# Prices and ranks of a hand-planned schedule: attention with mixed heads, then a squared-ReLU FFN

## The chip, the core and the metric

The kernel runs on one core of a Trainium2 chip. The core has a matrix engine (PE, with its weight loads shown as PEld), a vector engine (DVE), a scalar engine (ACT), a general engine (POOL), a queue engine that mostly issues DMAs (SP), and 16 DMA engines. Each engine works through its own instructions strictly in the order in which the program lists them, and waits at an instruction until its inputs and its buffers are there. The metric is the device time of one execution in microseconds; less is better.

## The reference

```python
scores = scale * np.matmul(q, k.transpose(0, 1, 3, 2))        # batch 8, heads 12, seq 448, head_dim 64
scores = np.einsum('bhij,hg->bgij', scores, w_pre)
scores = scores - np.max(scores, axis=-1, keepdims=True)
attn = np.exp(scores)
attn = attn / (np.sum(attn, axis=-1, keepdims=True) + 1e-09)
attn = np.einsum('bhij,hg->bgij', attn, w_post)
out = np.matmul(attn, v)
...
x = out.transpose(0, 2, 1, 3).reshape(B * S, H * D)           # 3584 x 768
h = np.maximum(x @ w_in, 0.0)                                 # 3584 x 2048
y = h * h @ w_out                                             # 3584 x 768
```

Heads are mixed before the softmax by w_pre (12 x 12) and after it by w_post. Then each of the 3584 tokens goes through a two-layer FFN with a squared ReLU.

## The kernel before

**Tiling.** Attention runs batch by batch. The 448 rows of a batch are cut into 45 chunks of about 10 query rows times 12 heads, so that a chunk fills 120 partitions. A chunk needs, in this order: a mix product of the scores with the w_pre pattern (L801, or L807 for the chunks of the first batch that mix q instead), a minimum on DVE (L812), an exponential on ACT (L815), a reciprocal on DVE (L821), a scaling of the w_post pattern on POOL (wq, L824), four products that both mix back and transpose (L831), and an eviction into `atb` by DVE or ACT (L485 or L487). Before that stand the scores (L679), their eviction into `snat`, and a DMA on SP that lays them out by chunk in `sch`. After it, the products with v (L876) fill `xt`.

**FFN.** Two batches share a block of 896 tokens, which is worked in units of 256 or 128 tokens. The first layer (L933, `mms` in `unit`) takes six products for each 128 hidden columns; DVE (L947) or ACT (L951) does the ReLU into `hr`; POOL squares it into `h2` (L954, at the rank FILL). The second layer (L972) takes 16 products for each group of 128 tokens and 384 output columns, in four pieces of four products; the groups are evicted into `osb`, of which there are two, and stored by SP (L996).

**The plan.** `Planner` simulates the engines while the program is built and writes down the order in which each picks its operations; that order is the program's. An operation has a price in ns for each engine that may do it, a rank `pri` (lower goes first) and dependencies. An engine that comes free takes the ready operation of lowest rank. Attention work ranks by chunk number (`n`), scores and relayouts ahead of it by AHEAD, most FFN work at FILL = 1e6, so that the FFN fills what attention leaves. An operation with two engines goes to whichever comes free first. Only the order reaches the chip; a price that differs from the chip's time makes an order that waits there.

**Near copies.** From the third batch on, q and k are loaded by POOL's DMAs into `qs` and `ks` (`load`, price 750), copied by `near` on POOL or DVE into `qn` and `kn` with the heads of a pair side by side (L610; `x_piece` makes six copies for each of two pieces of a batch, 72 in all), and then transposed by a DMA that SP issues (turn_k L623, turn_q L629) into the slots `kt` and `qz` that the scores read. A turn also waits until the slot's former scores are done. The copies rank `b * NCHUNK - 24 + 4.5 * g`, that is 24 chunks before their batch.

**Idle products.** At the start PE does products on zeros (L1183) where the plan leaves it idle, so that its clock stays up. They are planned before 9 us, and until 130 us wherever the planner's model of the clock is slow, or where PE's share of the last 3413 ns is under IDLE_LOW. The landings of the first loads of k, q and the last rows of q are planned by `first`, with a count of rows and ns a row.

Of the kernel before, what the change touches and what calls it, by code (L numbers as in the profile page):

```python
# [17 lines left out]
FT = DFF // 128  # L18
# [17 lines left out]
P_KEYS = S // NB  # L36
W2B = 2 * S
NSLOT = 2
NEAR, TURN_SP = {"POOL": 1000, "DVE": 270}, 1500
PIECE = NPAIR // 2  # L40
NE = 6
NSCH = 11
AHEAD = 7.4
FIFO = 50
IDLE_NS, IDLE_COLS, IDLE_FROM, IDLE_END, IDLE_LOW = 112, 256, 1300, 130000, 0.55
SPELL, PHASE, DROP, RISE = 3413, 1700, 0.4, 0.8
ROWS, COLS = 1, 2
TURN = 95
LATER = 2
GS, ONE = [(0, 1, 2)], [(0,), (1,), (2,)]  # L50
STAY = {ROWS: 2, COLS: 6}
HOLD = "g"
# [24 lines left out]
SOON = 0  # L77
# [42 lines left out]
class Planner:  # L120
# [8 lines left out]
    def add(self, eng, ns, pri, fn, deps=(), lat=60, bank=None, frees=None, mode=0):  # L129
        op = Op(eng if isinstance(eng, dict) else {eng: ns}, lat, pri, fn, list(deps), bank, frees, mode)  # L130
        self.ops.append(op)
        return op
# [169 lines left out]
def kernel(  # L302
# [189 lines left out]
    add = pl.add  # L492
    FILL = 1e6
    slots = {}
# [3 lines left out]
    def load(rows, each, pri, fn, deps):  # L498
        if len(loads) >= 7:
            deps = list(deps) + [loads[-7]]  # L500
        op = add("POOL", 750, pri, fn, deps, lat=850)
        done = pl.moved("LOAD", rows, each[0], each[1], 0, [op], 1500)
        loads.append(done)
        return done

    q_in, k_in, v_in = {}, {}, {}
    def keep(key, fn):
        def go(*got):
            for key_, slot in zip(key if isinstance(key, list) else [key], got):
                slots[key_] = slot  # L510
            fn(*got)
        return go
# [12 lines left out]
    h_op, sq_op, o_op, st_op = {}, {}, {}, {}  # L525
# [81 lines left out]
    tq_op, tk_op = {}, {}  # L607
# [4 lines left out]
    def x_piece(b, g):  # L612
        i = (2 * b + g) % NSLOT
        h0 = 2 * PIECE * g

        def pair_k(eng, a):
            near(eng, kn[:, :, 2 * a:2 * a + 2, :], ks[:, h0 + 2 * a:h0 + 2 * a + 2, :, :].rearrange("p h j d -> p j h d"))

        def pair_q(eng, a):
            near(eng, qn[:, :, 2 * a:2 * a + 2, :], qs[:, h0 + 2 * a:h0 + 2 * a + 2, :, :].rearrange("p h r d -> p r h d"))  # L620

        def turn_k():
            nc.sync.dma_start(  # L623
                out=kt[i][:, :, :, :].rearrange("p j a c -> p (j a) c"),
                in_=kn[:, :, :, :].rearrange("p j h d -> p (j h d)"), transpose=True,
            )

        def turn_q():
            nc.sync.dma_start(  # L629
                out=qz[i][:, :, :, :].rearrange("p r a c -> p (r a) c"),  # L630
                in_=qn[:, :, :, :].rearrange("p r h d -> p (r h d)"), transpose=True,
            )

        pri = b * NCHUNK - 24 + 4.5 * g
        old = used(b, g)
        ck = [
            add(NEAR, 0, pri, lambda eng, a=a: pair_k(eng, a), [k_in[b, g], tk_op.get(2 * b + g - 1)], lat=80)
            for a in range(PIECE)
        ]
        cq = [  # L640
            add(NEAR, 0, pri, lambda eng, a=a: pair_q(eng, a), [q_in[b, g], tq_op.get(2 * b + g - 1)], lat=80)
            for a in range(PIECE)
        ]
        sk = add("SP", 2300 if b == 2 else TURN_SP + 300, pri, turn_k, ck + old)
        sq = add("SP", 2000 if b == 2 else TURN_SP + 100, pri, turn_q, cq + old)
        k_ = tk_op[2 * b + g] = add("TURN", 1500, pri, lambda: None, [sk], lat=6000)
        q_ = tq_op[2 * b + g] = add("TURN", 1200, pri, lambda: None, [sq], lat=6000)
        for p in range(PIECE * g, PIECE * g + PIECE):
            ready[b, p] = [[k_]] + [[k_, q_]] * NJ
            got_op[b, p] = ck + cq  # L650
# [16 lines left out]
    def score(b, r, group):  # L667
# [13 lines left out]
        first = TAIL_FIRST if b == 0 and r == 0 else C0[r]  # L681
        pri = b * NCHUNK + first - AHEAD - 0.6 - (0.7 if r == 0 else 1.4) * (NPAIR - p)
        n = b * (NJ + 1) + r - 2
# [232 lines left out]
    def unit(pair, ui):  # L916
        a, z = units_of(pair)[ui]
        w = z - a
        nf = 512 // w
        ix = len(units)  # L920
        units.append((pair, ui))
        h2_ = h2[ix % 2]
        fill = FILL + 100 * ix
# [3 lines left out]
        prev = None  # L927
        for f0 in range(0, FT, nf):
            key = ("f", ix, "h", f0)
            for j in range(nf):  # L930
                def mms(slot, f0=f0, j=j):
                    for c2 in range(NPAIR):
                        nc.tensor.matmul(  # L933
                            slot[:, j * w:(j + 1) * w], lhsT=w1[c2][:, (f0 + j) * 128:(f0 + j + 1) * 128],
                            rhs=xt[:, c2, a:z], start=(c2 == 0), stop=(c2 == NPAIR - 1),
                        )
                if j == 0:
                    prev = add("PE", w * 2.55, fill + f0, keep(key, mms), xdeps + w1_in + [prev], lat=0, bank=key)
                else:
                    prev = add("PE", w * 2.55, 0, lambda key=key, mms=mms: mms(slots[key]), [prev], lat=0)  # L940
# [23 lines left out]
        for mt in range(w // 128):  # L964
            whole = not (z == W2B and mt == 1 and pair == B // 2 - 1)
            cuts = [0, 384, DMODEL] if whole else [0, 384, 640, DMODEL]
            for nt, (c0, c1) in enumerate(zip(cuts, cuts[1:])):
                key = ("f", ix, "o", mt, nt)
                for f0 in range(0, FT, 4):
                    def mms(slot, f0=f0, mt=mt, c0=c0, c1=c1):  # L970
                        for ft in range(f0, f0 + 4):
                            nc.tensor.matmul(  # L972
                                slot[:, 0:c1 - c0], lhsT=h2_[:, ft, mt * 128:(mt + 1) * 128],
                                rhs=w2[:, ft, c0:c1],
                                start=(ft == 0), stop=(ft == FT - 1),
                            )
                    if f0 == 0:
                        prev = add("PE", 12 + (c1 - c0) * 5 // 3, fill + 20 + 4 * mt + 2 * nt, keep(key, mms),
                                   [prev] + sq_op[ix][0:4 // nf] + w2_in[0:1 if ix < SOON else 4], lat=0, bank=key)
                    else:  # L980
                        prev = add("PE", 12 + (c1 - c0) * 5 // 3, FILL, lambda key=key, mms=mms: mms(slots[key]), [prev, w2_in[f0 // 4]] + sq_op[ix][0:(f0 + 4) // nf], lat=0)
                    o_op[ix].append(prev)
                end = add("WAIT%s" % str(key), 0, 0, lambda: None, [prev], lat=200)
                si = ix_store[0]

                def evac(eng, key=key, si=si, c0=c0, c1=c1):
                    copy(eng, osb[si % 2][:, c0:c1], slots[key][:, 0:c1 - c0])

                ev = add({"DVE": 80 + (c1 - c0) * 25 // 24, "ACT": 165 + (c1 - c0) * 5 // 7}, 0, 0, evac, [end, st_op.get(si - 2)] + ([m_op[n_] for n_ in direct] if si < 2 else []), lat=100, frees=key)
                evs = evs + [ev] if nt == 1 and whole else [ev]  # L990
                if nt == 1 or not whole:
                    done = []
                    for rows, dst, o in pieces(pair, a + mt * 128, None if whole else (c0, c1)):
                        side_ = not whole and rows <= CI
                        def store(dst=dst, o=o, rows=rows, si=si, e0=0 if whole else c0, e1=DMODEL if whole else c1, eng=nc.scalar if side_ else nc.sync):
                            eng.dma_start(out=dst, in_=osb[si % 2][o:o + rows, e0:e1])  # L996
                        done.append(add("ACT" if side_ else "SP", 510 if rows <= CI else 930, FILL, store, evs))
                    st_op[si] = pl.moved("DMA", 8, 140, 130, 0, done, 1500)
            if whole:
                ix_store[0] += 1  # L1000
# [28 lines left out]
    def first(us, rows, each):  # L1029
        return pl.moved("LOAD", rows, each, each, 0, [add("FIRST", 0, us, lambda: None, lat=1000 * us + 1600)], 1300)  # L1030

    tails0 = []
    for what, us in zip(LOADS0, FIRST_AT):
        if what[0] == "k":
            k_in[0, what[1]] = first(us, 28, 48)
        elif what[0] == "a":
            q_in[0, "a"] = first(us, 48, 30)
        elif what[0] == "q":
            q_in[0, what[1]] = first(us, 32, 36)
        elif what[0] == "t":  # L1040
            tails0.append(first(us, 24, 24))
    tail_in[0] = add("TAIL", 0, 0, lambda: None, tails0, lat=0)
    started = add("POOL", int(1000 * FIRST_AT[-1]) + 1400, -100, lambda: None)

# [20 lines left out]
    w2_in = [add("W2", 0, 0, lambda: None, lat=0) for i in range(4)]  # L1065
# [158 lines left out]
```

## Time and profile before

| what | value |
|---|---|
| runs shown, median | 581.34 us (580.34 to 581.96) |
| profiled execution | 582.53 us |
| its span | 580.8 us |
| mean granted PE clock | 0.997 |
| instructions of the span | 16782 |

The span runs from the first to the last instruction; the execution's time is longer by what lies around it. A row of the stretches gives the stretch, its length, the busy time of the engines in the order PE, PEld, DVE, ACT, POOL (instructions in brackets), the granted PE clock, the DMA share and GB/s. A row of the timeline gives start, duration, engine, line, operation, what is written and read, the count, and in square brackets the idle time before it with its releaser. A row of the waits gives the total, the times and the longest.

### The profile page before, as it was taken

The page shows a single profiled execution, that of the slowest core. Times are in us where ns is not written, and L with a number is a line of the kernel's source. Part 1 is how long each engine was busy: PE and PEld are TensorE (multiplying, and loading weights), DVE is VectorE, ACT ScalarE, POOL GpSimd, SP SyncE. Part 2 cuts the span into 40 slices and gives each one's busy share as a digit, 9 for nine tenths or more (in the row PEclk, how much of TensorE's full clock was granted, in tenths as well). Part 3 has the DMA queues.
Part 4 walks back from the last instruction along what each step waited for, and adds up shares of the span by engine and source line. Part 5 has one row for each costly group of instructions (what it writes and reads, how often), then busy time and mean ns, then how long its engine had stood idle before and what let it go on. Part 6 is the DMA issues. An engine that isn't in the chain of part 4 may idle for free.

```text
span 580.8 us, 16782 instructions
## 1 busy us (share of the span) xinstructions
PE 566.0 (97%) x5820; PEld 406.4 (70%) x5820; DVE 507.6 (87%) x1124; ACT 452.4 (78%) x1198; POOL 323.0 (56%) x593
## 2 busy tenths in 40 slices
PE   7989999999999898999999999999999999999997
PEld 4667666776677576767668677767768676767785
DVE  7999998999989899989898998999899988988442
ACT  5789989789888876888897888889798888887200
POOL 8357356655665267635776357734677344645441
PEclk9999999999999999999999999999999999999999
DMA  9999849954897449764498649954297545322021
GB/s 136 217 186 220 164 114 197 159 146 125 155 157 169 136 120 182 158 133 122 92 204 144 158 142 143 199 131 133 76 201 160 153 139 113 118 75 80 2 56 54
DMA packets 131810, 80.90 MB, mean 139 GB/s; under 512 B 59298, under 2 KB 126732, under 8 KB 131724
## 3 DMA queue, kind: packets, MB, share of 16 engines
q1 hardware_dynamic: 84892, 56.99, 40.1%
q0 software_dynamic: 46784, 22.81, 30.3%
q8 instruction: 45, 0.74, 0.5%
q14 instruction: 41, 0.34, 0.2%
q10 hardware_dynamic: 48, 0.02, 0.0%
HBM read 45.61 MB, written 11.01 MB: 98 GB/s over the span
## 4 chain that ended last, share of the span: by engine, by line
PE 84%; DMA 5%; DVE 5%; POOL 3%; issue 2%; ACT 1%; DVEq 0%; SPq 0%; POOLq 0%
PE bank L933 24%; PE bank L972 22%; PE bank L831 12%; PE bank L801 10%; PE bank L876 6%; PE bank L679 6%; DMA ks<-in_k_dram 2%; DMA sch<-snat 2%; DVE mn L812 1%; PE bank L807 1%; DVE atb L485 1%; DMA qs<-in_q_dram 1%; POOL wq L824 1%; DVE snat L485 1%; POOL ks L361 1%
## 5 line engine op out<-in xcount | busy, mean ns | idle before, releaser
L815 ACT ACTIVATE es<-bank,mn 120x448 bf16<-120x448 f32 x360 | 228.0, 641 | 50.5 <-DVE mn L812 45.7
L824 POOL TENSOR_SCALAR wq<-wback,rc 120x120 bf16<-120x120 f32 (+1 forms) x347 | 123.6, 369 | 158.1 <-DVE rc L821 93.7
L812 DVE TENSOR_REDUCE mn<-bank 120x1 f32<-120x448 f32 x360 | 209.2, 610 | 2.0 <-PE bank L801 1.8
L972 PE MATMUL bank<-w,h 128*128 128x384 bf16 (+2 forms) x912 | 173.0, 323 | 0.0
L933 PE MATMUL bank<-xt,w 128*128 128x256 bf16 (+1 forms) x1632 | 164.3, 253 | 0.8 <-ACT es L815 0.7
L954 POOL TENSOR_TENSOR h<-hr 128x512 bf16<-128x512 f32 x112 | 116.5, 1041 | 66.0 <-DVE hr L947 37.0
L933 PEld LDWEIGHTS <-w 128*128 128x128 bf16 x1632 | 136.1, 98 | 24.5 <-issue 3.9
L831 PEld LDWEIGHTS <-es 120*112 120x112 bf16 (+1 forms) x1440 | 107.9, 130 | 31.9 <-ACT es L815 6.3
L485 DVE CAST atb<-bank 112x480 bf16<-112x480 f32 (+2 forms) x188 | 114.6, 617 | 13.6 <-PE bank L831 11.6
L831 PE MATMUL bank<-wq,es 120*112 120x120 bf16 (+1 forms) x1440 | 118.3, 217 | 5.8 <-POOL wq L824 3.5
L972 PEld LDWEIGHTS <-h 128*128 128x128 bf16 x912 | 85.8, 97 | 54.1 <-issue 2.1
L487 ACT CAST atb<-bank 112x480 bf16<-112x480 f32 (+3 forms) x196 | 103.0, 538 | 12.0 <-PE bank L831 10.1
L801 PE MATMUL bank<-sch,wmix 120*128 120x448 bf16 x339 | 107.0, 354 | 0.7 <-DVE atb L485 0.5
L485 DVE CAST snat<-bank 128x448 bf16<-128x448 f32 x152 | 88.8, 613 | 3.6 <-PE bank L679 1.5
L487 ACT CAST snat<-bank 128x448 bf16<-128x448 f32 x172 | 84.4, 543 | 4.6 <-PE bank L679 3.3
L815 ACT ACTIVATION_READ_ACCUMULATOR es<-bank,mn 120x1 f32 x360 | 74.1, 206 | 0.0
L947 DVE TENSOR_SCALAR hr<-bank 128x512 f32<-128x512 f32 x80 | 55.0, 688 | 18.5 <-PE bank L933 15.1
L801 PEld LDWEIGHTS <-wmix 120*128 120x128 bf16 (+1 forms) x347 | 30.9, 98 | 21.4 <-issue 12.7
L876 PE MATMUL bank<-atb,vs 112*64 112x192 bf16 (+3 forms) x864 | 40.4, 250 | 0.0
L679 PE MATMUL bank<-kt,qz 64*128 64x448 bf16 x276 | 39.0, 357 | 0.8 <-DVE hr L947 0.6
L876 PEld LDWEIGHTS <-vs 112*64 112x64 bf16 x864 | 36.4, 110 | 3.4 <-issue 2.5
L485 DVE COPY osb<-bank 128x384 f32<-128x384 f32 (+2 forms) x32 | 17.3, 541 | 21.3 <-PE bank L972 18.2
(72 smaller groups left out, 307.1 us busy)
## 6 DMA issues: line engine op xcount, KB each, us to landing
sch<-snat SPq DMA_DIRECT2D x324, 105.0 KB
out_dram<-osb SPq DMA_DIRECT2D x22, 360.0 KB
vs<-in_v_dram POOLq DMA_DIRECT2D x16, 336.0 KB, 8.3
ks<-in_k_dram POOLq DMA_DIRECT2D x14, 336.0 KB, 9.5
qs<-in_q_dram POOLq DMA_DIRECT2D x14, 288.0 KB, 9.9
w<-in_moe_w_in_dram POOLq DMA_DIRECT2D x6, 512.0 KB, 14.6
w<-in_moe_w_out_dram POOLq DMA_DIRECT2D x4, 768.0 KB, 19.6
out_dram<-osb SPq DMA_DIRECT2D x8, 192.0 KB
```

Of the source, the lines that this page charges most:

```text
L485: nc.vector.tensor_copy(out=out_, in_=in_)
L487: nc.scalar.copy(out=out_, in_=in_)
L679: nc.tensor.matmul(slot[:, 0:S], lhsT=lhsT, rhs=kt[i][half, :, at_, :], start=True, stop=True)
L801: nc.tensor.matmul(slot[:, 0:S], lhsT=wm[0:rows, :], rhs=src[0:rows, :], start=True, stop=True,)
L812: nc.vector.tensor_reduce(out=mn[i][0:rows, :], in_=slots[mk][0:rows, 0:S], axis=AX.X, op=ALU.min)
L815: nc.scalar.activation(out=es[i][0:rows, 0:S], in_=slots[mk][0:rows, 0:S], func=ACT.Exp, scale=-1.0, bias=mn[i][0:rows, 0:1], accum_out=sm ...
L824: nc.gpsimd.tensor_scalar(out=wq[i][0:rows, :, 0:ns], in0=back[0:rows, :, 0:ns], scalar1=rc[i // 2][0:rows, i % 2:i % 2 + 1], scalar2=1.0, ...
L831: nc.tensor.matmul(slot[0:P_KEYS, jb * H * ns:(jb + 1) * H * ns], lhsT=es[i][0:rows, jb * P_KEYS:(jb + 1) * P_KEYS], rhs=wq[i][0:rows, :, ...
L876: nc.tensor.matmul(v_[64 * hh:64 * hh + 64, i, 0:x1 - x0], lhsT=vs[:, 2 * c2 + hh, jb, :], rhs=atb[half][:, jb, 2 * c2 + hh, x0:x1], start ...
L933: nc.tensor.matmul(slot[:, j * w:(j + 1) * w], lhsT=w1[c2][:, (f0 + j) * 128:(f0 + j + 1) * 128], rhs=xt[:, c2, a:z], start=(c2 == 0), sto ...
L954: nc.gpsimd.tensor_tensor(out=h2_[:, f0:f0 + nf, 0:w], in0=hr[gi % 2][:, :].rearrange("p (f c) -> p f c", f=nf), in1=hr[gi % 2][:, :].rear ...
L972: nc.tensor.matmul(slot[:, 0:c1 - c0], lhsT=h2_[:, ft, mt * 128:(mt + 1) * 128], rhs=w2[:, ft, c0:c1], start=(ft == 0), stop=(ft == FT - 1),)
```

## The change

Seven edits, none of which adds or takes away work of the reference's computation:

- the near copies rank at `NEAR_LAST` = 2e6 and cost 640 on POOL and 480 on DVE in the plan;
- FFN output products are planned in pieces of `OSTEP` = 2 products, each depending on the squares that it reads;
- scores and relayouts rank ahead by 7.6 chunks and not 7.4;
- idle products are planned where PE's share is under 0.62 and not 0.55;
- a DMA issue of `load` costs 830 and not 750 in the plan;
- the first loads of k cost 52 ns a row (48 before), of q 42 (36), of the last rows 30 (24), which moves their planned landings.

The first of these is two edits, of rank and of price.

```diff
-NEAR, TURN_SP = {"POOL": 1000, "DVE": 270}, 1500
+NEAR, TURN_SP = {"POOL": 640, "DVE": 480}, 1500
...
-AHEAD = 7.4
+AHEAD = 7.6
...
-IDLE_NS, IDLE_COLS, IDLE_FROM, IDLE_END, IDLE_LOW = 112, 256, 1300, 130000, 0.55
+IDLE_NS, IDLE_COLS, IDLE_FROM, IDLE_END, IDLE_LOW = 112, 256, 1300, 130000, 0.62
...
+NEAR_LAST = 2e6
+OSTEP = 2
...
-        op = add("POOL", 750, pri, fn, deps, lat=850)
+        op = add("POOL", 830, pri, fn, deps, lat=850)
...
-            add(NEAR, 0, pri, lambda eng, a=a: pair_k(eng, a), [k_in[b, g], tk_op.get(2 * b + g - 1)], lat=80)
+            add(NEAR, 0, NEAR_LAST, lambda eng, a=a: pair_k(eng, a), [k_in[b, g], tk_op.get(2 * b + g - 1)], lat=80)
...
-            add(NEAR, 0, pri, lambda eng, a=a: pair_q(eng, a), [q_in[b, g], tq_op.get(2 * b + g - 1)], lat=80)
+            add(NEAR, 0, NEAR_LAST, lambda eng, a=a: pair_q(eng, a), [q_in[b, g], tq_op.get(2 * b + g - 1)], lat=80)
...
-                for f0 in range(0, FT, 4):
+                for f0 in range(0, FT, OSTEP):
                     def mms(slot, f0=f0, mt=mt, c0=c0, c1=c1):
-                        for ft in range(f0, f0 + 4):
+                        for ft in range(f0, f0 + OSTEP):
...
                     if f0 == 0:
-                        prev = add("PE", 12 + (c1 - c0) * 5 // 3, fill + 20 + 4 * mt + 2 * nt, keep(key, mms),
-                                   [prev] + sq_op[ix][0:4 // nf] + w2_in[0:1 if ix < SOON else 4], lat=0, bank=key)
+                        prev = add("PE", (12 + (c1 - c0) * 5 // 3) * OSTEP / 4, fill + 20 + 4 * mt + 2 * nt, keep(key, mms),
+                                   [prev] + sq_op[ix][0:max(1, OSTEP // nf)] + w2_in[0:1 if ix < SOON else 4], lat=0, bank=key)
                     else:
-                        prev = add("PE", 12 + (c1 - c0) * 5 // 3, FILL, lambda key=key, mms=mms: mms(slots[key]), [prev, w2_in[f0 // 4]] + sq_op[ix][0:(f0 + 4) // nf], lat=0)
+                        prev = add("PE", (12 + (c1 - c0) * 5 // 3) * OSTEP / 4, FILL, lambda key=key, mms=mms: mms(slots[key]), [prev, w2_in[f0 // 4]] + sq_op[ix][0:(f0 + OSTEP + nf - 1) // nf], lat=0)
...
-            k_in[0, what[1]] = first(us, 28, 48)
+            k_in[0, what[1]] = first(us, 28, 52)
...
-            q_in[0, what[1]] = first(us, 32, 36)
+            q_in[0, what[1]] = first(us, 32, 42)
...
-            tails0.append(first(us, 24, 24))
+            tails0.append(first(us, 24, 30))
```

## The prediction

> **What bounds the kernel now.** I read the page's engine shares first, then the busy time of each engine in stretches, then the waits of TensorE (PE), and then the timeline around each place where PE stood still.
>
> ```profile
> span 580.8 us, 16782 instructions
> PE 566.0 (97%) x5820; PEld 406.4 (70%) x5820; DVE 507.6 (87%) x1124; ACT 452.4 (78%) x1198; POOL 323.0 (56%) x593
> ```
>
> PE is busy for 566.0 of 580.8 us, so 14.8 us of PE idle time is nearly all that another order of the same work can win. Where that idle time lies:
>
> ```profile
> 0.00:80.00 80.00, 72.72 (x893) 51.20 (x894) 73.86 (x193) 64.09 (x165) 46.52 (x86) 0.98 1.04 177
> 80.00:160.00 80.00, 79.90 (x831) 55.56 (x828) 74.87 (x164) 68.08 (x183) 47.63 (x90) 1.00 0.83 154
> 160.00:180.00 20.00, 19.48 (x206) 14.92 (x204) 18.16 (x43) 16.79 (x45) 14.49 (x26) 1.00 1.11 164
> 180.00:200.00 20.00, 18.42 (x165) 11.98 (x160) 17.30 (x39) 16.52 (x46) 6.20 (x16) 1.00 0.58 148
> ...
> 220.00:240.00 20.00, 18.48 (x167) 13.51 (x166) 19.11 (x39) 14.71 (x41) 14.69 (x26) 1.00 1.25 196
> 240.00:480.00 240.00, 240.00 (x2405) 171.86 (x2403) 219.37 (x476) 204.20 (x545) 138.61 (x259) 1.00 0.70 145
> ...
> 560.00:580.00 20.00, 17.02 (x141) 12.89 (x138) 6.54 (x11) 0.00 (x0) 6.87 (x7) 1.00 0.15 43
> ```
>
> The columns after the stretch are busy us of PE, PEld, DVE, ACT and POOL, and the first number after them is the granted PE clock. PE idles 7.28 us in the first 80 us, where DVE is busy for 73.86 of 80 and little FFN work is there to fill PE; 0.52 + 1.58 + 1.52 = 3.62 us between 160 and 240; nothing at all from 240 to 480; and 2.98 us before 580, with the 0.8 us after it. The end stays: ACT has nothing left there (0.00), PE has FFN products only, and then come the last eviction and store.
>
> Of the first 7.28 us, 1.06 us pass before the first product and 0.67 + 1.07 us are waits for q to land (both below); no order removes these. So a better order can win 3.62 us in the middle, 7.28 - 1.06 - 1.74 = 4.48 us at the start, and what a full clock at the start would give.
>
> **Part 1, near copies.** The diff lets the 72 copies of k and q into kn and qn rank behind everything (2e6, behind the squares' 1e6) and prices them 640 on POOL and 480 on DVE instead of 1000 and 270. No copy, turn or byte is added. Before:
>
> ```profile
> L610 DVE COPY kn<-ks x19: 271/295/2379, 102.2 to 448.1; 112x512 bf16<-112x512 bf16 x19
> L610 POOL COPY kn<-ks x17: 600/611/673, 101.4 to 429.7; 112x512 bf16<-112x512 bf16 x17
> L610 POOL COPY qn<-qs x20: 494/502/793, 101.9 to 449.3; 128x384 bf16<-128x384 bf16 x20
> L610 DVE COPY qn<-qs x16: 268/280/1298, 116.8 to 449.9; 128x384 bf16<-128x384 bf16 x16
> L954 POOL TENSOR_TENSOR h<-hr x112: 1030/1041/1079, 46.0 to 567.5; 128x512 bf16<-128x512 f32 x112
> ```
>
> A copy takes 500 to 610 ns on POOL. On DVE the median is 280 to 295, but single ones take up to 2379. The long ones show why:
>
> ```profile
> 225.91 0.50 POOL L610 COPY qn<-qs 128x384 bf16<-128x384 bf16 x1
> 226.03 2.38 DVE L610 COPY kn<-ks 112x512 bf16<-112x512 bf16 x1
> 226.36 0.81 POOL L361 DMA_DIRECT2D ks<-in_k_dram  x1
> 227.20 1.05 POOL L954 TENSOR_TENSOR h<-hr 128x512 bf16<-128x512 f32 x1
> ...
> 228.33 0.47 DVE L610 COPY qn<-qs 128x384 bf16<-128x384 bf16 x2
> ...
> 229.45 0.37 PE L679 MATMUL bank<-kt,qz 64*128 64x448 bf16 x2 [0.63 <-DVE hr L947]
> ...
> 230.01 0.37 PE L679 MATMUL bank<-kt,qz 64*128 64x448 bf16 x2 [0.20 <-DVE atb L485]
> ...
> 231.36 0.81 PE L933 MATMUL bank<-xt,w 128*128 128x256 bf16 x6 [0.69 <-ACT es L815]
> ```
>
> The copy that began at 226.03 ended at 228.41, just after POOL's run of copy, DMA issue and square ended at 228.25. DVE, in order, then had its maxima and evictions late, and PE stood still for 0.63 + 0.20 + 0.69 = 1.52 us, all that the stretch from 220 to 240 lacks. The same collision at another place cost PE nothing:
>
> ```profile
> 361.44 1.30 DVE L610 COPY qn<-qs 128x384 bf16<-128x384 bf16 x1
> 361.56 1.04 POOL L954 TENSOR_TENSOR h<-hr 128x512 bf16<-128x512 f32 x1
> ```
>
> With 640 for 1000 the planner sees POOL come free earlier and so gives it more of the copies; with 480 for 270 it gives DVE fewer of them in a row. Both prices are near what the rows show, so what follows on DVE and POOL is planned nearer to where it runs. I take this stall as gone, -1.5, and a half of the 0.52 between 160 and 180 (squares and wq behind three POOL copies) as gone too, -0.3. The other end: a piece of copies again meets a POOL run and costs PE 1.52 at one more place than now, +1.5.
>
> The Trainium skill, SBUF — State Buffer, section Who interferes with whom, says that a DVE copy in a two-port mode and any GpSimd instruction exclude each other, and the second waits for the whole of the first; the rows of 226 and 361 us agree. By that rule ranking copies behind squares speaks against the change, because a DVE copy then starts while POOL squares; that is the second rival below.
>
> What the moved copies pass: on POOL the squares (1.04 us each) and the loads; behind them on SP stand the turns that wait for them, and the relayout moves behind the turns. A few squares of delay make 2 to 4 us.
>
> ```profile
> 239.19 1.39 SPq L623 DMA_TRANSPOSE kt<-kn  x1
> ```
> ```profile
> 250.88 0.72 DVE L610 COPY qn<-qs 128x384 bf16<-128x384 bf16 x2
> 252.23 1.75 SPq L629 DMA_TRANSPOSE qz<-qn  x1
> ```
>
> The copies that ended at 228.80 were turned only at 239.19, since the slot was not free: 10 us of cover, and the delay costs nothing. At the second piece the copies end at 251.60 and the turn goes out at 252.23; there the cover is 0.63 us, so a delay of one square costs 0.4 and of two 1.45, as a wait of SP, then of the sch moves behind it, then of PE's mixes; I take 1.0 for a piece that it hits, and none in the sum.
>
> **Part 2, output products in pieces of two.** The same 912 products are planned in about twice as many pieces, 326 instead of 652 each; the first piece of a 256-wide unit needs one square instead of two. No instruction is added, and a weight load goes with every product already, so the direct cost is nil. The gain is that a score, mix or attention product that becomes ready waits for two products (0.33 us) rather than four. Its price is the cushion: a product put 0.16 us earlier on average in the plan leaves less room for a late DVE or POOL. I take 0 for these two, with -1.0 to +1.0 as bounds, an estimate: a little under a third of all that PE now waits for wq, its commonest wait:
>
> ```profile
> PE bank L831 <- POOL wq L824: 3.5, 6, 0.9
> ```
>
> What the pieces do change is where an output group ends, and with that the one wait of 1.58 us near 196:
>
> ```profile
> 187.69 7.78 SPq L707 DMA_DIRECT2D sch<-snat  x9
> 195.52 1.93 SPq L996 DMA_DIRECT2D out_dram<-osb  x3
> ...
> 197.46 0.56 DVE L485 COPY osb<-bank 128x384 f32<-128x384 f32 x1 [2.52 <-DMA out_dram<-osb]
> ...
> 198.07 0.42 PE L831 MATMUL bank<-wq,es 120*112 120x120 bf16 x4 [1.58 <-DVE osb L485]
> ```
>
> An eviction to osb had to wait for a store that SP issued at 195.52, behind nine relayout moves, and DVE stood in it for 2.52 us. Output pieces that can end at other times make the coincidence unlikely to recur at this place, but nothing forbids it at another of the 28 row tiles: -0.8, a half, with -1.6 and +1.6 as ends.
>
> **Part 3, first landings and idle products.** The planner's landings of the three parts of q move from 9.38, 10.54 and 11.69 us (start 2.9, then rows times ns, plus 1.3) to 9.91, 11.26 and 12.60. The trace has:
>
> ```profile
> 1.06 3.81 PE L1183 MATMUL bank<-still 128*128 128x256 bf16 x17 [1.06 <-DVE still L367]
> ...
> 9.44 0.53 PE L547 MATMUL bank<-ident,qs 128*64 128x128 bf16 x12 [0.67 <-DMA qs<-in_q_dram]
> 11.04 0.53 PE L547 MATMUL bank<-ident,qs 128*64 128x128 bf16 x12 [1.07 <-DMA qs<-in_q_dram]
> 12.17 0.85 PE L547 MATMUL bank<-ident,qs 128*64 128x128 bf16 x12
> ```
>
> The old plan was 0.06 to 0.50 early, the new one is 0.22 to 0.47 late: it now sees gaps before q and may fill them. This matters because of the clock (same columns as above):
>
> ```profile
> 9.00:12.40 3.40, 1.77 (x34) 1.07 (x36) 3.12 (x12) 2.23 (x6) 2.98 (x5) 0.97 1.61 167
> 12.40:15.60 3.20, 3.20 (x26) 1.67 (x23) 2.94 (x11) 2.91 (x7) 2.53 (x4) 0.50 1.41 203
> ```
>
> PE was busy for 52% of the 3.4 us up to 12.40, and then had a clock of 0.50 for 3.2 us; at full clock that work takes 1.6 us less. The new plan puts some 3 more idle products before the third part of k and, by the threshold 0.62, up to 4 before the third part of q: 4 times 0.112 us raise the share to at most 65%. Whether that holds the clock no row shows, and DVE (2.94 of 3.20) would not follow all of the 1.6. I take -0.6, with -1.6 and 0 as ends. More idle products may fall after that; each is 0.11 us, and ten in PE's way would be +1.1, but they are planned only where PE idles, so I count none.
>
> The Trainium skill, TensorE: Matmul & The Clock Gate, section What's actually happening, has a free-running window of 3413 ns and a half rate after an idle one; the 3.2 us at 0.50 agree, and by it the loss is either taken whole or not at all.
>
> **Part 4, load price 830 and AHEAD 7.6.** A DMA issue on POOL was priced 750:
>
> ```profile
> L350 POOL DMA_DIRECT2D qs<-in_q_dram x17 | 14.6, 864 | 0.0
> ...
> L361 POOL DMA_DIRECT2D ks<-in_k_dram x17 | 13.4, 791 | 0.9 <-POOLq L1208 0.9
> ```
>
> 830 lies between the two. Scores and relayouts rank 0.2 of a chunk earlier, about 0.3 us (360 chunks in some 545 us are 1.5 us each). Neither adds work. Against the 4.48 us of idle at the start I take -0.5, ends -1.5 and +1.5, since every such edit also redraws all that follows.
>
> **The sum.** -1.5 - 0.3 - 0.8 - 0.6 - 0.5 = -3.7 us. The profiled execution took 582.53 us, 1.7 more than its span, so it would become 578.8; the median of the three runs is 581.34, 1.2 below the profiled one, so on their scale the forecast is **577.6**. With the first and the third term at nothing it is 579.9; with parts 2 and 3 at their better ends (0.8 and 1.0 more) it is 575.8: the forecast's own range.
>
> **The rivals.**
> - *The stalls change places.* All orders after about 9 us are redrawn, and the three stalls of 0.52, 1.58 and 1.52 were accidents; if as many new ones come as go, only the start helps: 581.3 - 0.6 = 580.7. For it speaks that PE is busy for 240.00 of 240 us from 240 on, so that only accidents tell two plans apart there and before; against it, that the prices move towards the rows.
> - *DVE copies locked behind squares (slower).* With copies ranked behind squares, POOL is in a square or a run of them whenever copies are left, and a copy that DVE takes then waits 1 to 2 us, as at 361 and 226. It decides once more than about three of the 12 pieces put PE in the position of 228 us: four such stalls for the one now are +3 x 1.52 = 4.6, less 0.8 and 0.6 from parts 2 and 3: 584.5. Against it: at 361 us the same lock cost PE nothing, and the planner now charges 480.
> - *The turns come late.* A copy that starves behind squares and loads holds SP, the sch moves behind it and so the mixes; at the second pieces there is no cover. At one wait of 1.0 us in each of six batches less the 1.5 of part 1 and the 0.6 of part 3: 581.3 + 6.0 - 2.1 = 585.2. Against it: POOL idles 44%.
> - *More than forecast.* The clock stays full, and the middle loses all 3.62 us and the start 1.5: 581.3 - 1.6 - 3.6 - 1.5 = 574.6.
>
> **How the numbers follow.** Forecast 0.46, stalls change places 0.20, copies locked 0.15, turns late 0.07, more than forecast 0.12. What a measurement of this kernel can tell from no change is 0.3%, 1.7 us: faster is below 579.6, slower above 583.1. Faster: 0.12, most of the forecast (0.42) and a part of the second case (0.04), 0.58. Slower: 0.19 of the two slow rivals and 0.04 of the second case, 0.23. The rest, 0.19, is within. The range of 574.0 to 584.5 takes in 0.46 + 0.20, the half of the copies' case that lies at or below its price (0.07) and three quarters of the case above the forecast (0.09): 0.82.
>
> **What would show it.** Right: PE at 20.00 in the stretches from 160 to 240; no DVE copy over 1.5 us; more than 37 of the 72 copies on POOL; the granted clock in 0 to 20 us above 0.91. Wrong: PE waits on DVE evictions just after DVE copies that end with a square; turns that SP waits for with PE's mixes behind; a new wait on out_dram<-osb. A PE idle time that stays at 14.8 us with the same clock at the start would make the whole forecast wrong.

## The result and the profile after

The changed kernel takes 579.19 us (median of 17 executions, 578.11 to 582.76), the kernel before, run beside it, 583.5 us (17 executions, 580.34 to 587.91). The ratio is 0.9935, with an interval of 0.9914 to 0.9956: 3.8 us less. (The two medians by themselves lie 4.3 us apart.) The forecast was 3.7 us less on a before of 581.34, so 577.6; the measured time is 1.6 us above that, where the kernel before, timed again, took 2.2 us more than 581.34.

First the engine shares of the changed kernel's page, then its busy time in the stretches that were read before (PE, PEld, DVE, ACT, POOL, granted clock).

```profile
span 580.5 us, 16838 instructions
...
PE 567.8 (98%) x5840; PEld 408.5 (70%) x5840; DVE 504.6 (87%) x1116; ACT 446.0 (77%) x1182; POOL 334.6 (58%) x617
```

```profile
0.00:80.00 80.00, 73.98 (x891) 52.08 (x891) 72.81 (x188) 60.42 (x158) 45.70 (x84) 0.96 1.02 175
80.00:160.00 80.00, 77.51 (x816) 54.74 (x815) 73.71 (x161) 65.73 (x176) 48.99 (x95) 1.00 0.76 143
160.00:180.00 20.00, 20.00 (x191) 14.96 (x189) 18.56 (x41) 16.68 (x46) 15.03 (x27) 1.00 1.18 196
180.00:200.00 20.00, 20.00 (x202) 13.84 (x201) 19.23 (x46) 17.46 (x50) 11.32 (x26) 1.00 0.70 152
...
220.00:240.00 20.00, 20.00 (x187) 14.56 (x185) 19.23 (x44) 17.52 (x46) 17.24 (x28) 1.00 1.26 180
240.00:480.00 240.00, 239.84 (x2404) 171.56 (x2402) 216.17 (x468) 203.47 (x539) 144.15 (x274) 1.00 0.70 146
```

The 3.62 us of idle time between 160 and 240 are gone (20.00 in each of the three stretches that had it, 19.98 from 200 to 220). Against that, the stretch from 80 to 160 now lacks 2.49 us where it lacked 0.10. The first 80 us have 1.3 us less idle time, but no more work is done in them. These are the idle products alone, first in the kernel before and then in the changed kernel:

```profile
20.00:80.00 60.00, 0.95 (x8) 0.75 (x9) 1.00 1.00 184
20.00:80.00 60.00, 2.73 (x16) 1.47 (x16) 1.00 0.98 180
```

PE spends 1.78 us more on products on zeros between 20 and 80 us. With the idle products taken off its count (29 and 8 before, 32 and 16 now), PE has begun 856 products by 80 us in the kernel before and 843 in the changed one.

In this execution the span is only 0.3 us shorter than before, and it took 582.39 us, above the median by 3.2. It is one of the five in which the clock was lost for longest, and that happened at the start. These are stretches of the changed kernel there, and PE's timeline:

```profile
9.00:12.40 3.40, 1.31 (x15) 0.63 (x15) 3.23 (x14) 0.70 (x2) 3.34 (x6) 0.87 1.66 178
12.40:15.60 3.20, 3.20 (x35) 1.71 (x34) 2.88 (x9) 2.70 (x7) 1.91 (x4) 0.50 1.41 206
15.60:20.00 4.40, 4.40 (x23) 2.27 (x21) 3.50 (x10) 3.31 (x9) 0.00 (x0) 0.68 1.12 210
```

```profile
5.86 0.58 PE L549 MATMUL bank<-ident,ks 112*64 112x112 bf16 x16
...
9.27 0.53 PE L549 MATMUL bank<-ident,qs 128*64 128x128 bf16 x12 [0.38 <-DMA qs<-in_q_dram]
11.49 0.34 PE L1048 MATMUL bank<-wmix,perm 120*120 120x120 bf16 x1 [1.70 <-DVE wmix L467]
11.96 0.56 PE L681 MATMUL bank<-kt,qz 64*128 64x448 bf16 x2
12.44 0.85 PE L549 MATMUL bank<-ident,qs 128*64 128x128 bf16 x12
```

With q planned to land later, the planner put the product of the mix pattern (L1048) ahead of the second part of q; PE stood at it for 1.70 us, until DVE had made wmix. The granted clock lacks 0.13, 0.50 and 0.32 of the full one in the three stretches, so it was at half for some 6.9 us (0.13 x 3.4 x 2 + 3.2 + 0.32 x 4.4 x 2); by the same reckoning it was 3.4 us in the kernel before (0.03 x 3.4 x 2 + 3.2). But this is not so in every execution. The clock that an execution was granted on average tells how long it was halved: 0.997 in the profile of before, 0.994 in this one. Sorted by it, over all executions of this study:

| kernel | clock 0.999 or 1.000 | 0.996 to 0.998 | 0.994 or less |
|---|---|---|---|
| before, 100 executions beside the experiments | 35, median 581.9 us | 32, 583.7 | 33, 585.4 |
| changed, 17 | 11, 578.9 | 1, 578.8 | 5, 581.0 |

So the difference of the medians, 4.3 us, has two parts: 3.0 us remain between executions that were granted 0.999 or more (581.9 to 578.9), and 1.3 us come from a clock that is lost less often. This split is rough, since the executions of before in the table were not timed beside those of the changed kernel. Nor does any profile show where the 3.0 us are: the only one of the changed kernel is of the slower kind.

The start decides how often the clock is lost. The changed kernel and the six kernels below that have its order of PE in the first 20 us kept 0.999 or more in 52 of 85 executions (the one with added idle products is not among them); the kernel before and the five that have its order there, in 62 of 160. One reason why the same order keeps the clock in one execution and not in the next shows in a profile of a variant with the changed kernel's start (the near copies undone), which was granted 0.999:

```profile
6.60 0.96 PE L549 MATMUL bank<-ident,ks 112*64 112x112 bf16 x16
...
11.52 0.26 PE L1048 MATMUL bank<-wmix,perm 120*120 120x120 bf16 x1 [0.31 <-DVE wmix L467]
```

The first sixteen products of k took 0.96 us here and 0.58 above. PE worked at a slower pace until about 9.4 us, was later with everything, and so stood before the mix pattern for 0.31 us and not for 1.70. Of the 14 profiles of this study, five have this late start, and none of them lost the clock afterwards; of the nine with the early one, seven did. The granted clock of the rows is 1.00 in these first microseconds either way, so a mean of 0.999 does not mean that the start was fast.

### The profile page after: what moved, and what is told of

Read it like the earlier page. It is cut to its first block, busy times and chain, and to the rows that moved or that the text cites. A ratio compares the mean times of both kernels' runs of the same rounds, so it can differ in the third digit from the quotient of the medians.

```text
span 580.5 us, 16838 instructions
## 1 busy us (share of the span) xinstructions
PE 567.8 (98%) x5840; PEld 408.5 (70%) x5840; DVE 504.6 (87%) x1116; ACT 446.0 (77%) x1182; POOL 334.6 (58%) x617
## 4 chain that ended last, share of the span: by engine, by line
PE 91%; DVE 3%; DMA 3%; POOL 1%; issue 1%; ACT 1%; DVEq 0%; POOLq 0%
PE bank L935 25%; PE bank L974 24%; PE bank L833 13%; PE bank L803 11%; PE bank L681 7%; PE bank L878 7%; DMA sch<-snat 3%; PE bank L809 2%; PE bank L1185 1%; DVE mn L814 1%; POOL wq L826 1%; PE bank L549 0%; DVE atb L487 0%; DVE snat L487 0%; ACT es L817 0%
## 5 line engine op out<-in xcount | busy, mean ns | idle before, releaser
L974 PE MATMUL bank<-w,h 128*128 128x384 bf16 (+2 forms) x912 | 184.2, 323 | 0.0
L833 PEld LDWEIGHTS <-es 120*112 120x112 bf16 (+1 forms) x1440 | 109.8, 129 | 30.5 <-issue 7.1
L974 PEld LDWEIGHTS <-h 128*128 128x128 bf16 x912 | 84.2, 98 | 55.2 <-issue 7.3
L833 PE MATMUL bank<-wq,es 120*112 120x120 bf16 (+1 forms) x1440 | 119.7, 217 | 2.2 <-POOL wq L826 1.9
L487 DVE CAST atb<-bank 112x480 bf16<-112x480 f32 (+3 forms) x192 | 113.0, 600 | 7.8 <-PE bank L833 5.2
L489 ACT CAST atb<-bank 112x480 bf16<-112x480 f32 (+1 forms) x192 | 103.7, 551 | 16.9 <-PE bank L833 15.8
L803 PE MATMUL bank<-sch,wmix 120*128 120x448 bf16 x339 | 108.5, 353 | 2.9 <-DVE snat L487 2.1
L823 DVE RECIPROCAL rc<-sm 120x2 f32<-120x2 f32 x180 | 27.8, 155 | 8.3 <-ACT es L817 6.3
```

Source lines behind the costliest of these rows:

```text
L487: nc.vector.tensor_copy(out=out_, in_=in_)
L489: nc.scalar.copy(out=out_, in_=in_)
L803: nc.tensor.matmul(slot[:, 0:S], lhsT=wm[0:rows, :], rhs=src[0:rows, :], start=True, stop=True,)
L833: nc.tensor.matmul(slot[0:P_KEYS, jb * H * ns:(jb + 1) * H * ns], lhsT=es[i][0:rows, jb * P_KEYS:(jb + 1) * P_KEYS], rhs=wq[i][0:rows, :, ...
L974: nc.tensor.matmul(slot[:, 0:c1 - c0], lhsT=h2_[:, ft, mt * 128:(mt + 1) * 128], rhs=w2[:, ft, c0:c1], start=(ft == 0), stop=(ft == FT - 1),)
```

## The experiments

Four runs undo one part of the change, four make one part alone, three shift a price by a nanosecond, one fills the idle time before the mix pattern. Each was timed beside the kernel before.

**Parts undone.** The near copies' old rank and prices:

```diff
-NEAR, TURN_SP = {"POOL": 640, "DVE": 480}, 1500
+NEAR, TURN_SP = {"POOL": 1000, "DVE": 270}, 1500
...
-            add(NEAR, 0, NEAR_LAST, lambda eng, a=a: pair_k(
+            add(NEAR, 0, pri, lambda eng, a=a: pair_k(
```

> The changed kernel with the near copies' old rank and prices (1000/270). Terms theory (the gains of the parts add up): the copies' 1.8 us come back, ratio to before 0.9935 + 0.0031 = 0.9966, and copies over 1 us on DVE return. Clock theory (the gain is the clock that holds at the start in most executions): the ratio stays 0.9935, since the first 20 us are unchanged. Redraw theory (each edit reorders everything and the stalls are a new draw): anywhere between 0.990 and 1.003, with new PE waits at places that neither kernel has.

Pieces of four:

```diff
-OSTEP = 2
+OSTEP = 4
```

> The changed kernel with FFN output products in pieces of four again. Terms theory: 0.8 us come back, 0.9949. Clock theory: 0.9935 and the same first 20 us. Redraw theory: between 0.990 and 1.003, with other places of PE's waits after 80 us.

Old landings and threshold:

```diff
-... IDLE_LOW = 112, 256, 1300, 130000, 0.62
+... IDLE_LOW = 112, 256, 1300, 130000, 0.55
...
-            q_in[0, what[1]] = first(us, 32, 42)
+            q_in[0, what[1]] = first(us, 32, 36)
```

(and 48 for k, 24 for the last rows).

> The changed kernel with the old landings of the first loads and IDLE_LOW 0.55. Terms theory: 0.6 us come back, 0.9945. Clock theory: nearly the whole gain is lost, 0.998 to 1.000, with a granted clock of 0.5 for 3 us after 12 us in nearly every execution. Redraw theory: between 0.990 and 1.003.

Old AHEAD and load price:

```diff
-AHEAD = 7.6
+AHEAD = 7.4
...
-        op = add("POOL", 830, pri, fn, deps, lat=850)
+        op = add("POOL", 750, pri, fn, deps, lat=850)
```

> The changed kernel with AHEAD 7.4 and a price of 750 for a load's DMA issue. Terms theory: 0.5 us come back, 0.9944. Clock theory: 0.9935. Redraw theory: between 0.990 and 1.003, with the new wait on a relayout near 100 us gone or moved, as ranks of relayouts change.

**Parts alone**, each the kernel before with one of the four edits.

> The kernel before with the new rank and prices of the near copies alone. Terms theory: -1.8 us, ratio 0.997; the DVE copy of 2.4 us near 226 and the 1.52 us of PE idle time behind it are gone. Redraw theory: between 0.990 and 1.005; other PE waits after 100 us.

> The kernel before with FFN output products in pieces of two alone. Terms theory: -0.8 us, 0.9986, the wait on the store near 196 gone. A rival, that finer pieces cut the cushion: slower, 1.000 to 1.003, with PE waiting longer for wq than the 3.5 us of before. Redraw theory: between 0.990 and 1.005.

> The kernel before with the new landings and IDLE_LOW 0.62 alone. Terms theory: -0.6 us, 0.999. Clock theory: most of the gain, 0.994 to 0.996, and a clock of 1.0 after 2 us in most executions. Redraw theory: between 0.990 and 1.005.

> The kernel before with AHEAD 7.6 and a price of 830 for a load's DMA issue alone. Terms theory: -0.5 us, 0.999. Clock theory: 1.000. Redraw theory: between 0.990 and 1.005.

Measured, as ratios to before with their intervals:

| part | undone in the changed kernel | alone in the kernel before |
|---|---|---|
| near copies | 1.0024 (0.9997 to 1.005) | 1.004 (1.0013 to 1.0067) |
| pieces of two | 0.9995 (0.9966 to 1.0023) | 0.9975 (0.9954 to 0.9996) |
| landings, idle products | 1.000 (0.9969 to 1.003) | 1.0034 (1.0006 to 1.0062) |
| AHEAD, load price | 0.9991 (0.997 to 1.0011) | 0.9984 (0.9969 to 1.000) |
| all four together | | 0.9935 (0.9914 to 0.9956) |

The terms theory falls. Two parts alone do win their terms (1.5 us for 0.8, 0.9 for 0.5), but the other two lose time. Alone, the parts add up to +0.40 - 0.25 + 0.34 - 0.16 = +0.33% or 1.9 us slower, where all together are 3.8 us faster; and undoing any one of them costs 0.56 to 0.89%, about all of the 0.65% that the four win. The clock theory falls as the main cause as well: the kernel with the landings undone and the kernel with them alone are both no faster than before, although the latter was granted 0.999 or more in 7 of its 8 executions. What fits is the redraw theory, that each edit gives another order; its ranges were so wide, 0.990 to 1.005, that it could hardly have failed here.

The mechanisms that the prediction named are there, but they strike where the draw puts them. In the kernel with the near copies' part alone, the lock between DVE and POOL is worse than before, even in the profiled execution, at 581.03 us the fastest of its twelve. From its timeline:

```profile
228.30 1.06 POOL L956 TENSOR_TENSOR h<-hr 128x512 bf16<-128x512 f32 x1
...
228.75 3.37 DVE L612 COPY kn<-ks 112x512 bf16<-112x512 bf16 x1
229.32 0.70 POOL L826 TENSOR_SCALAR wq<-wback,rc 120x120 bf16<-120x120 f32 x2
...
230.00 1.03 POOL L956 TENSOR_TENSOR h<-hr 128x512 bf16<-128x512 f32 x1
...
230.98 0.82 POOL L363 DMA_DIRECT2D ks<-in_k_dram  x1
231.84 0.84 POOL L826 TENSOR_SCALAR wq<-wback,rc 120x120 bf16<-120x120 f32 x2
...
233.23 0.35 PE L803 MATMUL bank<-sch,wmix 120*128 120x448 bf16 x1 [1.01 <-DVE snat L487]
```

The DVE copy that began at 228.75 ended at 232.12, when POOL's unbroken run of two squares, two scalings and a DMA issue had ended at 231.80; PE then waited 1.01 us for DVE. This is the second rival, that copies behind squares get locked, in one place. The kernel with the near copies undone shows that it is not what decides. Its copies, by engine (shortest, median, longest ns):

```profile
L612 POOL COPY kn<-ks x22: 601/613/727, 103.7 to 448.3; 112x512 bf16<-112x512 bf16 x22
L612 DVE COPY qn<-qs x20: 268/276/520, 107.1 to 451.4; 128x384 bf16<-128x384 bf16 x20
...
L612 POOL COPY qn<-qs x16: 493/504/561, 106.4 to 448.9; 128x384 bf16<-128x384 bf16 x16
L612 DVE COPY kn<-ks x14: 271/285/740, 118.6 to 448.9; 112x512 bf16<-112x512 bf16 x14
```

34 copies on DVE and none longer than 740 ns, and yet its median of 585.37 us is one of the two longest of all. Nor does the idle time of PE show it: its page has PE busy for 570.8 of 583.6 us, so PE idles 2.0 us less than in the kernel before (12.8 and 14.8), and the span is 2.8 us longer. But 11.2 us of its busy time are idle products, where the kernel before has 7.1; with them counted as idle, PE lacks 24.0 us and 21.9. In the kernel with the landings alone the third rival appears, turns that hold SP. From its timeline:

```profile
112.45 3.70 SPq L631 DMA_TRANSPOSE qz<-qn  x1
116.20 5.90 SPq L709 DMA_DIRECT2D sch<-snat  x7
...
120.81 0.53 ACT L489 CAST snat<-bank 128x448 bf16<-128x448 f32 x1 [2.46 <-DMA sch<-snat]
...
121.40 0.35 PE L681 MATMUL bank<-kt,zt 128*128 128x448 bf16 x1 [1.83 <-ACT snat L489]
```

A turn took SP for 3.70 us, seven relayouts came out after it, the eviction into `snat` waited for one that still read the buffer, and PE stood for 1.83 us.

**One nanosecond.** Is the order of the changed kernel good because its prices are truer, or is it one lucky draw? These edits say nothing new to the planner and still change the order, though not from the start: in the traces the first two leave the changed kernel's order as it is until about 192 and 208 us, and the third that of the kernel before until about 95 us.

```diff
-NEAR, TURN_SP = {"POOL": 640, "DVE": 480}, 1500
+NEAR, TURN_SP = {"POOL": 641, "DVE": 481}, 1500
```

> The changed kernel with 641 and 481 for 640 and 480, one nanosecond a copy, which changes nothing that the change is about but gives another order from about 100 us on. If the gain lies in truer prices and finer pieces, the ratio stays at 0.992 to 0.996. If it is one favourable draw among orders, it falls back to 0.998 to 1.003, as with each of the four parts undone, with PE waits of 0.5 to 2 us at places that the changed kernel does not have.

```diff
-            rl = add({"ACT": 500, "DVE": 590}, 0, 0, relu,
+            rl = add({"ACT": 500, "DVE": 591}, 0, 0, relu,
```

> The changed kernel with a price of 591 for 590 ns for the ReLU on DVE: another draw of the same kind, another order from the first FFN work on. Truer prices: 0.992 to 0.996. Draw: 0.997 to 1.003.

```diff
-        op = add("POOL", 750, pri, fn, deps, lat=850)
+        op = add("POOL", 751, pri, fn, deps, lat=850)
```

> The kernel before with 751 for 750 ns for a load's DMA issue. Truer prices theory: 1.000, as one nanosecond is nothing. Draw theory: between 0.994 and 1.004, and not like the kernel before in the places of its waits after 40 us.

Measured: 0.9935 (0.9909 to 0.9961), 0.9977 (0.9949 to 1.0006) and 0.9974 (0.9946 to 1.0003). The first neighbour keeps the whole gain, as truer prices would, the second 0.23 of 0.65%, as a draw would, and the neighbour of the kernel before wins 0.26% by itself (its interval reaches 1.0003). Between executions with a granted clock of 0.999 or more, timed side by side, the medians are 579.9 (8 executions), 582.2 (6) and 582.1 (5) where before has 582.1 (10): there the second neighbour keeps nothing, and the third wins nothing. The first two lie 2.2 us apart (580.12 and 582.37 over all executions) and differ by one nanosecond in each case. In the profile of the second, PE lacks 2.96 us from 240 to 480, where the changed kernel lacks 0.16. So a nanosecond can move the time by some 0.4%, and this noise of orders is larger than any single term of the prediction's sum. The mean ratio of the changed kernel and its two neighbours is 0.9949, that of the kernel before and its neighbour 0.9987: 0.38% or 2.2 us between them, from five orders, which is no proof that truer prices are worth anything, the less as the two neighbours share the changed kernel's first third.

**The idle time before the mix pattern.** In the changed kernel with nothing replanned:

```diff
     def w_turn(slot):
+        for _ in range(13):
+            stand(slot, 0)
         nc.tensor.matmul(
```

> The changed kernel with 13 more idle products (1.5 us) right before the product that waits for the mix pattern near 11.5 us, where PE stood idle for 1.7 us; the plan and every other order are the same. If that idle time is what drops the clock, the granted clock after 2 us is 1.0 in every execution (the changed kernel lost it in 5 of 17, for 2.3 us at the median) and the ratio goes from 0.9935 to 0.991 to 0.993, a median near 578.7 us where before is 583.4. If the clock is lost by chance of the window all the same, the ratio stays and some executions keep a mean clock of 0.993.

Measured: 578.7 us (577.96 to 579.98, 11 executions), ratio 0.9908 (0.9879 to 0.9937), the fastest kernel here; its interval still meets the changed kernel's. Its mean granted clock was 0.999 or 1.000 in all 11. Its timeline and stretches at the start:

```profile
6.59 0.96 PE L549 MATMUL bank<-ident,ks 112*64 112x112 bf16 x16
...
11.17 0.50 PE L549 MATMUL bank<-ident,qs 128*64 128x128 bf16 x12
11.61 1.59 PE L1187 MATMUL bank<-still 128*128 128x256 bf16 x13
13.04 0.22 PE L1050 MATMUL bank<-wmix,perm 120*120 120x120 bf16 x1
```

```profile
9.00:12.40 3.40, 3.40 (x56) 2.61 (x53) 3.03 (x12) 1.93 (x4) 2.96 (x6) 1.00 1.61 165
12.40:15.60 3.20, 3.20 (x47) 2.01 (x44) 2.24 (x9) 1.98 (x5) 2.49 (x4) 1.00 1.42 200
```

PE is busy from 9.00 to 15.60 and the clock stays at 1.00. This profile does not show the products at work, though: it is one with the late start (0.96 us for the sixteen products of k), which keeps the clock without them. What speaks is the count: 11 of 11 executions kept it, where 52 of 85 with the same start did without them. So the idle time before the product of the mix pattern, where DVE was late, is what the clock of the changed kernel was lost by. Between executions that were granted 0.999 or more the kernel is no faster than the changed one (578.7 against 578.9): these products buy only the certainty.

## Why the prediction was right, and where it was not

- **What bounds the kernel** held only in part. The 3.62 us between 160 and 240 went, against 2.4 us that came between 80 and 160. But the idle time that the prediction read off the page, 14.8 us, is less than what PE lacks, since idle products count as busy there: PE spends 10.2 us on them in the changed kernel and 7.1 in the kernel before. With them PE lacks 22.9 and 21.9 us in the two profiles, so the fall of the idle time from 14.8 to 12.7 us is no work done earlier.
- **The size of the sum** held, -3.7 against -3.8, and this was luck. The range of 574.0 to 584.5 took in the kernel before as well, so to land in it says little. The split did not hold: the step that failed is the addition itself. The prediction gave each edit its own stall to remove; the runs show that the near copies and the landings, which were to win 1.8 and 0.6 us, cost 0.40 and 0.34% alone, that the other two win somewhat more than their terms (0.25 and 0.16%), and that none can be taken out without the gain.
- **Part 1, near copies**: the stall at 228 us is gone in the changed kernel, and 61 of the 72 copies are on POOL as forecast (33 of kn and 28 of qn below). But -1.5 was put to the wrong cause: with this part alone PE loses 2.51 of the 20 us from 220 to 240, more than the 1.52 of before, and its ratio is 1.004. The longest DVE copy of the changed kernel, 1.48 us, stayed just under the 1.5 us that were to show the forecast right, and from 240 to 480, where it stands, PE lacks 0.16 us in all.

```profile
L612 POOL COPY kn<-ks x33: 600/613/663, 106.4 to 448.7; 112x512 bf16<-112x512 bf16 x33
L612 POOL COPY qn<-qs x28: 493/508/531, 109.7 to 450.8; 128x384 bf16<-128x384 bf16 x28
L612 DVE COPY qn<-qs x8: 279/430/1482, 109.8 to 451.6; 128x384 bf16<-128x384 bf16 x8
```
```profile
220.00:240.00 20.00, 17.49 (x157) 12.61 (x156) 18.45 (x36) 14.71 (x38) 16.04 (x24) 1.00 1.35 185
```

The first fence is the changed kernel, the second the kernel with the near copies' part alone.

- **Part 2, pieces of two**: forecast -0.8, alone -0.25% or 1.5 us (0.9954 to 0.9996); the wait on the store near 196 is gone. The cushion that finer pieces cut cost little: with them alone PE waits 3.9 us for wq, before it was 3.5.

```profile
PE bank L833 <- POOL wq L826: 3.9, 8, 0.9
```

- **Part 3, landings**: the -0.6 has the right sign for the clock and is too small (1.3 us of the difference of the medians), and its working was wrong. There were no added products between the parts of q; PE's share from 9.0 to 12.4 fell to 1.31 of 3.40 us in the profiled execution, 39%, and not up to 65%, since the wait for q was replaced by the wait for the mix pattern. The clock of the first 20 us was 0.83 there, and not above 0.91 as the prediction asked for. That the clock is nevertheless lost in fewer executions follows the start (52 of 85 kept it, against 62 of 160); which start an execution gets, the early or the late one, is left open. The prediction put more idle products after that at nothing: 17 more came after 20 us, and PE spent 2.84 us more on them up to 160. What they cost was not measured.
- **Part 4** took -0.5 as the worth of any redraw; alone it was -0.16% or 0.9 us, more than its term, with an interval that reaches 1.000.
- **The rivals.** "The stalls change places" describes what happens to every variant, with the size of the draw that it lacked: up to some 0.4% for a nanosecond. A new stall did come in the changed kernel, in the place of those removed:

```profile
100.45 1.16 DVE L487 CAST snat<-bank 128x448 bf16<-128x448 f32 x2 [2.88 <-DMA sch<-snat]
101.13 0.35 PE L803 MATMUL bank<-sch,wmix 120*128 120x448 bf16 x1 [2.09 <-DVE snat L487]
```

An eviction into `snat` waited 2.88 us for a relayout that still read it, and PE 2.09 us behind it. The locked copies and the late turns each cost PE time in a variant, not in the changed kernel.

What stays open is why this order in particular is good, and whether most orders near it would be as good: two neighbours of it and one of the kernel before are too few to tell truer prices from a lucky draw.

## What to carry to other kernels

Where a planner writes out the order and PE has no slack, test an edit against edits that mean nothing (a nanosecond in a price): if those move the time as much, the edit's own mechanism has not been measured, however well its stall is seen to vanish. A lower idle time of PE is no proof either, where idle products fill it. Read terms of such a sum as a bound on what is there to win, not as parts that add. A wait that leaves PE idle at the start is worth filling with idle products directly in front of the instruction that waits, since the planner's view of landings is not where PE will stand.

## What the runs showed of the hardware

- The same program is granted a different clock from one execution to the next: of 100 executions of the kernel before, 35 kept 0.999 or more, 33 had 0.994 or less, and the medians lie 3.5 us apart (581.9 and 585.4). In the changed kernel it is lost by PE's idle time around 10 us: with that filled, 11 of 11 executions kept 0.999 or more.
- PE comes to its full pace at one of two times. Sixteen products of k took 0.58 us early in nine profiles and about 0.96 us in five, with the granted clock of the rows at 1.00 in all of them; the five kept the clock afterwards, seven of the nine lost it for a time.
- A DVE copy can stand through several POOL instructions in a row, DMA issues among them: 2.38 us in the kernel before and 3.37 us in the variant, which ended 0.16 and 0.32 us after POOL's run. It is not always so: in the kernel before, three copies that DVE began at 313.53 had ended by 315.05, while POOL went on from its square at 314.68 with scalings until 315.54. What tells the two apart is open.
